# Two columns of the second feed-forward weight fetched by rows, around the first weight, in a decode step with cached attention

## The chip, the cores and the metric

The kernel runs on one core of a Trainium2 chip. The metric is the device time of one execution in microseconds (us); lower is better. TensorE multiplies matrices, VectorE (DVE), ScalarE (ACT) and GpSimd (POOL) work element by element, and SyncE (SP) issues all the transfers between the main memory and the on-chip memory here. Sixteen DMA engines carry these transfers. The on-chip memory has 128 partitions, which below are also called rows, since a row of a packed weight lies in one partition.

## The reference

One decoding step for four sequences: an adaptive layer norm that is steered by `c`, attention over a cache of 4096 keys and values with 32 heads of 128, a second adaptive layer norm, and a feed-forward block with SiLU.

```python
mod = (_silu(c) @ w_mod).reshape(c.shape[0], 6, 1, -1)
sa, ca, ga, sb, cb, gb = (mod[:, 0], mod[:, 1], mod[:, 2], mod[:, 3], mod[:, 4], mod[:, 5])
h = _layernorm(x) * (1 + ca) + sa
q = (h @ wq)                                   # (4, 32, 1, 128) after the reshape
scores = einsum("bhqd,bhkd->bhqk", q, k_cache) * 128 ** -0.5
o = einsum("bhqk,bhkd->bhqd", softmax(scores), v_cache)
x = x + ga * (o.reshape(4, 1, 4096) @ wo)
h = _layernorm(x) * (1 + cb) + sb
x = x + gb * (_silu(h @ w1) @ w2)              # w1: 512 x 1792, w2: 1792 x 512
```

All numbers are 32-bit floats. The two caches are 256 MiB each and are read once.

## The kernel before

The work is cut into N = 32 steps; a step is four heads of one sequence. For each step the keys (8 MB) and the values (8 MB) come into the on-chip memory, each into one of three `Slot`s of 8 MB that go round. In a step, VectorE and GpSimd multiply the keys by the query (`mult`, L280) and VectorE sums them (`red`, L285); the largest score is found (`rowmax`, `bmax`, `negmax`), ScalarE takes the exponentials (`softexp`, L307), and the sum over the values is shared by GpSimd (`vmult`) and TensorE (`pv`, L348). In the last two steps `first(n)` is 0, so that `pv` takes all 32 groups of the values, 64 matmul instructions.

After the last step's `pv` the closing work follows, in this order on TensorE:

- `project_a()` (L423): the output projection of the first half of the heads, from `wat`, the first RA x D = 8192 elements of each row of the slot that holds `wo`.
- `gather(NT - 1, 1)` (its matmul is L375), then `project(TA, NT - 1)` (L428) with three blocks of `wot`, 6144 elements a row, then `spread(NT - 1)` on VectorE, and `project(NT - 1, NT)` (L428) with the last block, 2048 elements a row.
- L500 and L501 copy the sum, four small matmuls spread it (L504), the residual is added, and the second layer norm follows (`layernorm_mod`). `busy` (L497) issues matmuls whose result nobody reads.
- L515 multiplies by the first feed-forward weight `w1t`, SiLU follows, and VectorE transposes the result (L186).
- L525 multiplies by the second weight `w2t`: NI = 14 columns of D = 512 elements a row (256 KB each over the 128 rows), added up in one accumulator `pf`. Each column takes 8 matmul instructions in the trace. Then L529, L530 and the output's transfer (L531).

The tile framework runs with a manual schedule: each engine carries out its instructions in the order in which the program text issues them. Waits are derived from the data: an instruction that reads a part of a tile waits for the transfer that writes that part, and for the whole of this transfer.

All transfers are issued by SP, nearly all through the helper `fetch` (L85), which cuts a row at the given places and issues one transfer of 128 rows for each piece. Each transfer reports on a semaphore; eight of them go round, so SP issues a transfer only when the one eight places before it has landed. The transfers at the end are, in the order of issue: the last keys in two halves, the last values, `wo` in three pieces (8192, 6144 and 2048 elements a row; the call is in the loop, L444), then `w12`, in which `w1` (4 x 1792 elements a row) and `w2` (14 x 512) lie one behind the other. `w12` (L476) comes in nine pieces: the first three quarters of `w1`, its last quarter, and `w2` by columns 0 to 4, 5 to 7, 8 and 9, and then one each for 10, 11, 12 and 13. The slot of `w12` is free once the last keys have been summed, and its first transfers are issued at 1278.9 us.

Of the kernel before, what the change touches and what calls it, by code (L numbers as in the profile page):

```python
# [17 lines left out]
def kernel(  # L18
# [10 lines left out]
    nc = tc.nc  # L29
    P = 128  # L30
    B, H, S, Dh = kc.shape
    D = wo.shape[1] * P // (H * Dh)
    F = w12.shape[1] * P // (2 * D)
# [8 lines left out]
    RA = Dh // QA  # L42
# [5 lines left out]
    R = Dh // QW  # L48
    NK = D // P
    NI = F // P  # L50
# [7 lines left out]
    SLOT = NJ * Dh  # L58
# [7 lines left out]
    def psum(shape, tag, bufs):  # L66
        return ps.tile(shape, F32, tag=tag, name=tag, bufs=bufs)
# [15 lines left out]
    def fetch(t, src, *cuts):  # L83
        for lo, hi in zip(cuts, cuts[1:]):
            nc.sync.dma_start(t[:, lo:hi], src[:, lo:hi])  # L85

    kt, vt = {}, {}

# [6 lines left out]
    def load_k(n, *cuts):  # L95
        load(kt, kc, "k", n, *cuts)

    def load_v(n):
        load(vt, vc, "v", n)
# [143 lines left out]
    for k in range(NK):  # L243
        for ch in range(H * Dh // CW):
            i, g = divmod(ch, G)
            nc.tensor.matmul(
                pq[i][W * g : W * (g + 1), :], hT[:, k, :], wqt[:, k, ch * CW : (ch + 1) * CW],
                start=k == 0, stop=k == NK - 1,
# [4 lines left out]
    for i in range(2):  # L253
        for u in range(HP):
# [3 lines left out]
                start=i + u == 0, stop=i == 1 and u == HP - 1,  # L258
# [6 lines left out]
    def make_qb(n):  # L265
        if n % B == 0:
            m = work.tile([P, B, Dh], F32, tag="o", name=f"qm{n}", bufs=1)
            for b in range(B):
                nc.scalar.activation(m[:, b, :], qn, AF.Copy, scale=sel[:, n + b : n + b + 1])  # L269
            p = psum([P, B, Dh], "q", 2)  # L270
            nc.tensor.matmul(p, blk.rearrange("p i x -> p (i x)"), m, start=True, stop=True)  # L271
            for b in range(B):
                qb[n + b] = p[:, b, :]
        qw[n] = work.tile([P, Dh], F32, tag="qw", name=f"qw{n}")
        nc.scalar.activation(qw[n], qb[n], AF.Copy)  # L275
# [3 lines left out]
    def mult(eng, src, n, lo, hi):  # L279
        eng.tensor_mul(  # L280
            kt[n][:, lo:hi, :], kt[n][:, lo:hi, :], src[n].unsqueeze(1).to_broadcast([P, hi - lo, Dh])
        )

    def red(n, lo, hi):
        nc.vector.tensor_reduce(sc[n][:, lo:hi], kt[n][:, lo:hi, :], axis=AX.X, op=ALU.add)  # L285

    def rowmax(n):
        nm[n] = work.tile([P, 1], F32, tag="rm", name=f"rm{n}")
        nc.vector.tensor_reduce(nm[n], sc[n], axis=AX.X, op=ALU.max)  # L289

    def bmax(n):
        p = psum([P, P], "mx", 2)
        nc.tensor.transpose(p, nm[n].to_broadcast([P, P]), ident)  # L293
        nm[n] = p

    def negmax(n):
        m = work.tile([P, HP], F32, tag="hx", name=f"hx{n}")
        nc.vector.tensor_reduce(m, nm[n].rearrange("p (i x) -> p i x", i=HP), axis=AX.X, op=ALU.max)  # L298
        nc.vector.tensor_mul(m, m, hn)
        nm[n] = work.tile([P, 1], F32, tag="nm", name=f"nm{n}")  # L300
        nc.vector.tensor_reduce(nm[n], m, axis=AX.X, op=ALU.add)  # L301

    def softexp(n):
        t, b = divmod(n, B)
        if b == 0:
            rs[t] = work.tile([P, B], F32, tag="rs", name=f"rs{t}")
        nc.scalar.activation(sc[n], sc[n], AF.Exp, bias=nm[n], accum_out=rs[t][:, b : b + 1])  # L307
        for h in range(2):
            f = first(n) if h == 0 else 0
            m = HG - f  # L310
            nc.gpsimd.tensor_mul(  # L311
                pz[h][:, f * W : HG * W].rearrange("p (g x) -> p g x", g=m)[:, :, E:].rearrange("p g (i j) -> p g i j", i=HP),
                sc[n][:, JJ * (HG * h + f) : HG * JJ * (h + 1)].rearrange("p (g j) -> p g j", j=JJ)
                .unsqueeze(2).to_broadcast([P, m, HP, JJ]),
                hm.unsqueeze(1).unsqueeze(3).to_broadcast([P, m, HP, JJ]),
            )

    def first(n):
        return NV // JJ if n < N - 2 else 0
# [9 lines left out]
    def vsum(n):  # L329
        t, b = divmod(n, B)  # L330
        q, a = divmod(b, 2)
        o = (1 - a) * E
        nc.tensor.matmul(  # L333
            po[t, q][0:W, :], hs[:, o : o + W], vt[n][:, :JJ, :].rearrange("p j d -> p (j d)"),
            start=False, stop=a == 1,
        )
# [42 lines left out]
    def norm(t):  # L379
        p = psum([P, B], "mx", 2)  # L380
        if t < TA:
            g = slice(W * t, W * (t + 1))
            nc.tensor.matmul(p[g], b8.rearrange("p i x -> p (i x)"), rs[t], start=True, stop=True)
            rd[t] = work.tile([P, B, QA], F32, tag="ra", name="ra", bufs=1)
            m = work.tile([P, B], F32, tag="dx", name="dx")
            nc.vector.reciprocal(m[g], p[g])
            nc.vector.tensor_mul(
                rd[t][g], m[g].unsqueeze(2).to_broadcast([W, B, QA]),
                dqm[g].unsqueeze(1).to_broadcast([W, B, QA]),
            )  # L390
            return
        nc.tensor.matmul(p, blk.rearrange("p i x -> p (i x)"), rs[t], start=True, stop=True)
        m = work.tile([P, B], F32, tag="dx", name="dx")
        nc.vector.tensor_mul(m, p, xm)
        rd[t] = work.tile([P, 2], F32, tag="rd", name="rd")
        nc.vector.tensor_reduce(rd[t][:, 0:1], m, axis=AX.X, op=ALU.add)
        nc.vector.reciprocal(rd[t][:, 1:2], rd[t][:, 0:1])

    def spread(t):
        if t < TA:  # L400
            g = slice(W * t, W * (t + 1))
            v = work.tile([P, B, QA, RA], F32, tag="o", name="v", bufs=1)
            nc.vector.tensor_mul(
                v[g], od[t][g].rearrange("p b (q r) -> p b q r", q=QA),
                rd[t][g].unsqueeze(3).to_broadcast([W, B, QA, RA]),
            )
            nc.vector.tensor_reduce(oa[g], v[g].rearrange("p b q r -> p r b q"), axis=AX.X, op=ALU.add)
            return
        on = work.tile([P, R, QW], F32, tag="lnu", name="on", bufs=1)
        nc.vector.tensor_scalar(  # L410
            on, od[t].rearrange("p (x r) -> p r x", r=R), rd[t][:, 1:2], None, op0=ALU.mult
        )
        ot = work.tile([P, R, W], F32, tag="o", name="ot", bufs=1)
        nc.vector.transpose(ot, on)
        nc.vector.tensor_copy(oz[:, t - TA], ot[:, :, :B])
# [19 lines left out]
    for n in range(N):  # L435
        t, b = divmod(n, B)
        if n < N - 2:
            load_k(n + 1)
        elif n == N - 2:
            load_k(n + 1, 0, NJ // 2, NJ)  # L440
        else:
            so = Slot("wo")
            wat, wot = so.take(RA, D), so.take(NT - TA, R, D)
            fetch(so.t, wo, 0, RA * D, SLOT - R * D, SLOT)  # L444
        sc[n] = work.tile([P, NJ], F32, tag="sc", name=f"sc{n}")
        if n + 1 < N:
            mult(nc.gpsimd, qw, n, 0, NA)
            mult(nc.vector, qb, n, NA, NJ)
            make_qb(n + 1)
            if n and first(n - 1):  # L450
                vsum(n - 1)
            red(n, NA, NJ)
        else:
            for lo in (0, NJ // 2):
                mid, hi = lo + NL // 2, lo + NJ // 2
                mult(nc.gpsimd, qw, n, lo, mid)
                mult(nc.vector, qb, n, mid, hi)
                red(n, mid, hi)
        if n + 1 < N:
            red(n, 0, NA)  # L460
        else:
            for lo in (0, NJ // 2):
                red(n, lo, lo + NL // 2)
        rowmax(n)
        bmax(n)
        negmax(n)
        if t and b == 1:
            spread(t - 1)
        softexp(n)
        if n + 1 < N:  # L470
            load_v(n + 1)
        else:
            s2 = Slot("w12")
            w1t = s2.take(NK, F)
            w2t = s2.take(NI, D)
            fetch(s2.t, w12, 0, 3 * F, *(NK * F + i * D for i in (0, 5, 8, 10, 11, 12, 13, 14)))  # L476
        if b == B - 1:
            norm(t)
        vmult(n)
        pv(n)  # L480
        if n and b == 0:
            gather(t - 1, 1)
        if b == 2:
            gather(t, 0)
# [28 lines left out]
    for k in range(NK):  # L513
        for g in range(G):
            nc.tensor.matmul(  # L515
                ph[W * g : W * (g + 1), :], h2T[:, k, :], w1t[:, k, g * FG : (g + 1) * FG],
                start=k == 0, stop=k == NK - 1,
# [2 lines left out]
    silu2(hid, th, ph)  # L520
    transposed(hidT, hid, NI)
    pf = psum([P, P], "po", 2)
    for i in range(NI):
        for g in range(G):
            nc.tensor.matmul(  # L525
                pf[W * g : W * (g + 1), :], hidT[:, i, :], w2t[:, i, g * P : (g + 1) * P],
                start=i == 0, stop=i == NI - 1,
            )
    nc.vector.tensor_mul(y, gb, pf)  # L529
    nc.vector.tensor_add(y, y, x1)  # L530
# [43 lines left out]
```

## Time and profile before

| | |
|---|---|
| time, median of 3 runs | 1320.01 us (1319.31 to 1320.38) |
| the profiled execution's own time | 1319.19 us |
| its span in the profile | 1317.4 us |
| busy: TensorE, VectorE, ScalarE, GpSimd | 377.2, 1017.4, 51.5, 842.8 us |
| moved by the DMA engines | 567.65 MB, mean 431 GB/s |
| mean granted TensorE clock | 0.611 of full speed |

Times in the profile count from the span's start. "L423 PE" is line 423 of the kernel on TensorE's matmul side, PEld its weight loads, PEldq the sequencer in front of them, SPq SP's own queue. A row of the timeline has start, duration, engine, line, operation, output <- input, shape and count, and in brackets the engine's idle time before it and what ended it. A row of busy time by stretches has the stretch, its length, busy time and count of PE, PEld, DVE, ACT and POOL, the granted TensorE clock, the busy share of the 16 DMA engines and the GB/s. A row of issues has the transfer, how often, its size and the time from issue to landing. A row of waits has who waited for whom, the total, the number of times and the longest. A piece of the chain of work that ended last has start, duration and what it was.

### The profile page before, as it was taken

The page shows a single profiled execution, that of the slowest core. Times are in us where ns is not written, and L with a number is a line of the kernel's source. Part 1 is how long each engine was busy: PE and PEld are TensorE (multiplying, and loading weights), DVE is VectorE, ACT ScalarE, POOL GpSimd, SP SyncE. Part 2 cuts the span into 40 slices and gives each one's busy share as a digit, 9 for nine tenths or more (in the row PEclk, how much of TensorE's full clock was granted, in tenths as well). Part 3 has the DMA queues.
Part 4 walks back from the last instruction along what each step waited for, and adds up shares of the span by engine and source line. Part 5 has one row for each costly group of instructions (what it writes and reads, how often), then busy time and mean ns, then how long its engine had stood idle before and what let it go on. Part 6 is the DMA issues. An engine that isn't in the chain of part 4 may idle for free.

```text
span 1317.4 us, 5420 instructions
## 1 busy us (share of the span) xinstructions
PE 377.2 (29%) x2114; PEld 94.6 (7%) x2114; DVE 1017.4 (77%) x361; ACT 51.5 (4%) x164; POOL 842.8 (64%) x227
## 2 busy tenths in 40 slices
PE   3421133223123232212332321332331233222138
PEld 1100000000000000000000000000000000000013
DVE  2378877777987777898777788777779877777982
ACT  1100000000000000000000000000000000000001
POOL 0236687666678666668866666876666787666650
PEclk9755566665566666556666555666655666655569
DMA  9999999999999999999999999999999999999998
GB/s 414 440 420 444 432 430 438 428 438 437 424 442 438 424 438 436 432 438 433 432 436 430 433 440 430 434 436 434 436 430 438 434 431 436 432 432 438 424 434 342
DMA packets 11433, 567.65 MB, mean 431 GB/s; under 512 B 1280, under 2 KB 1296, under 8 KB 2192
## 3 DMA queue, kind: packets, MB, share of 16 engines
q1 hardware_dynamic: 11408, 567.31, 99.5%
q8 instruction: 17, 0.28, 0.1%
q14 instruction: 8, 0.07, 0.0%
HBM read 567.30 MB, written 0.01 MB: 431 GB/s over the span
## 4 chain that ended last, share of the span: by engine, by line
DVE 36%; DMA 35%; POOL 19%; another core or an unknown queue 3%; PE 3%; issue 2%; ACT 1%; DVEq 0%; POOLq 0%; ACTq 0%
DMA k<-in_A_k_cache_dram 31%; DVE sc L285 21%; DVE k L280 14%; POOL v L327 9%; POOL v L323 8%; DMA w<-in_B_w_dram 3%; PE po L333 2%; DMA wm<-in_head_dram 1%; POOL pz L311 1%; POOL k L280 1%; ACT sc L307 1%; PE mx L293 1%; DVE hx L298 0%; DVE rm L289 0%
## 5 line engine op out<-in xcount | busy, mean ns | idle before, releaser
L285 DVE TENSOR_REDUCE sc<-k 128x88 f32<-128x11264 f32 (+2 forms) x66 | 553.1, 8422 | 1.1
L280 DVE TENSOR_TENSOR k<-k,q 128x11264 f32<-128x11264 f32 (+1 forms) x33 | 378.4, 11468 | 214.7 <-DMA k<-in_A_k_cache_dram 214.7
L280 POOL TENSOR_TENSOR k<-k,qw 128x5120 f32<-128x5120 f32 (+1 forms) x33 | 356.3, 10799 | 39.1 <-DMA k<-in_A_k_cache_dram 39.1
L311 POOL TENSOR_TENSOR pz<-sc,hm 128x128 f32<-128x128 f32 (+1 forms) x64 | 31.5, 512 | 376.9 <-ACT sc L307 376.9
L348 PE MATMUL po<-v,pz 128*32 128x512 f32 x1568 | 241.9, 781 | 44.9 <-POOL pz L311 44.8
L327 POOL TENSOR_TENSOR v<-v 128x2048 f32<-128x2048 f32 (+2 forms) x90 | 244.6, 2718 | 7.1
L323 POOL TENSOR_TENSOR v<-v,sc 128x4096 f32<-128x4096 f32 x30 | 210.9, 7031 | 0.0
L293 PE MATMUL mx<-ident,rm 128*128 128x128 f32 x32 | 14.5, 453 | 612.7 <-DVE rm L289 612.7
L333 PE MATMUL po<-v,hs 128*32 128x512 f32 x60 | 57.4, 1060 | 235.0 <-POOL v L327 235.0
L348 PEld LDWEIGHTS po<-v,pz 128*32 128x32 f32 x1568 | 56.6, 139 | 208.6 <-issue 156.2
L293 PEld LDWEIGHTS mx<-ident,rm 128*128 128x128 f32 x32 | 5.8, 181 | 664.9 <-issue 503.3
L307 ACT ACTIVATE sc<-sc,nm 128x128 f32<-128x128 f32 x32 | 12.8, 401 | 667.9 <-DVE nm L301 667.9
L275 ACT ACTIVATE qw<-q 128x128 f32<-128x128 f32 x32 | 8.9, 277 | 481.8 <-DVE k L280 454.2
L298 DVE TENSOR_REDUCE hx<-mx 128x4 f32<-128x128 f32 x32 | 9.3, 292 | 19.7 <-PE mx L293 19.7
L333 PEld LDWEIGHTS po<-v,hs 128*32 128x32 f32 x60 | 5.4, 140 | 257.9 <-POOL v L327 257.9
L359 DVE TENSOR_TENSOR o<-po,jm 128x512 f32<-128x512 f32 x16 | 10.9, 682 | 8.1 <-PE po L348 8.1
L365 DVE TENSOR_REDUCE s<-o 128x128 f32<-128x512 f32 x16 | 16.7, 1043 | 0.6
L199 PE MATMUL q<-wm 128*32 128x512 f32 x48 | 8.8, 665 | 18.8 <-DVE wm L183 18.8
L269 ACT ACTIVATE qm<-qn,sel 128x128 f32<-128x128 f32 x32 | 10.2, 390 | 31.2 <-PE od L370 27.7
L271 PE MATMUL q<-qm,blk 128*128 128x512 f32 x16 | 8.7, 625 | 7.2 <-ACT qm L269 7.2
L189 POOL COPY wm<-wm 128x16 f32<-128x16 f32 x1 | 0.2, 211 | 16.0 <-DMA wm<-in_head_dram 16.0
L183 DVE SCALAR_TENSOR_TENSOR wm<-wm 128x16 f32<-128x16 f32 x1 | 0.2, 189 | 12.8 <-ACT wm L182 12.8
(113 smaller groups left out, 153.2 us busy)
## 6 DMA issues: line engine op xcount, KB each, us to landing
k<-in_A_k_cache_dram SPq DMA_DIRECT2D x2, 4096.0 KB, 22.3
wm<-in_head_dram SPq DMA_DIRECT2D x1, 6160.0 KB, 17.6
wo<-in_A_wo_dram SPq DMA_DIRECT2D x1, 4096.0 KB, 26.8
wo<-in_A_wo_dram SPq DMA_DIRECT2D x1, 3072.0 KB, 33.7
w<-in_B_w_dram SPq DMA_DIRECT2D x1, 2688.0 KB, 23.8
w<-in_B_w_dram SPq DMA_DIRECT2D x1, 1280.0 KB, 28.1
wo<-in_A_wo_dram SPq DMA_DIRECT2D x1, 1024.0 KB, 35.7
w<-in_B_w_dram SPq DMA_DIRECT2D x4, 256.0 KB, 17.5
```

The lines of the kernel that those rows point to most:

```text
L269: nc.scalar.activation(m[:, b, :], qn, AF.Copy, scale=sel[:, n + b : n + b + 1])
L280: eng.tensor_mul(kt[n][:, lo:hi, :], kt[n][:, lo:hi, :], src[n].unsqueeze(1).to_broadcast([P, hi - lo, Dh]))
L285: nc.vector.tensor_reduce(sc[n][:, lo:hi], kt[n][:, lo:hi, :], axis=AX.X, op=ALU.add)
L293: nc.tensor.transpose(p, nm[n].to_broadcast([P, P]), ident)
L307: nc.scalar.activation(sc[n], sc[n], AF.Exp, bias=nm[n], accum_out=rs[t][:, b : b + 1])
L311: nc.gpsimd.tensor_mul(pz[h][:, f * W : HG * W].rearrange("p (g x) -> p g x", g=m)[:, :, E:].rearrange("p g (i j) -> p g i j", i=HP), sc[n ...
L323: nc.gpsimd.tensor_mul(vt[n][:, :NV, :], vt[n][:, :NV, :], sc[n][:, :NV].unsqueeze(2).to_broadcast([P, NV, Dh]))
L327: nc.gpsimd.tensor_add(vt[n][:, :m, :], vt[n][:, :m, :], vt[n][:, m : 2 * m, :])
L333: nc.tensor.matmul(po[t, q][0:W, :], hs[:, o : o + W], vt[n][:, :JJ, :].rearrange("p j d -> p (j d)"), start=False, stop=a == 1,)
L348: nc.tensor.matmul(po[t, q][W * g : W * (g + 1), :], pz[h][:, o : o + W], vt[n][:, JJ * j : JJ * (j + 1), :].rearrange("p j d -> p (j d)") ...
L359: nc.vector.tensor_mul(o, po[t, q].rearrange("p (j d) -> p j d", j=JJ), jm.unsqueeze(2).to_broadcast([P, JJ, Dh]))
L365: nc.vector.tensor_reduce(s, o.rearrange("p j d -> p d j"), axis=AX.X, op=ALU.add)
```

## The change

Three places change.

1. A helper `by_rows` issues transfers of whole columns of `w2` by groups of rows: each transfer takes a number of consecutive rows of one column. Column 12 comes so in transfers of 30, 42, 36 and 20 rows, issued ahead of `w1`; column 13 in transfers of 52, 44, 18, 8 and 6 rows, issued behind `w1`. The other twelve columns follow as before in transfers of 128 rows, now cut as 0 to 2, 3 to 5, 6 and 7, and then one each for 8, 9, 10 and 11. In all, `w12` comes in 18 transfers instead of nine.
2. `wo` comes in two transfers (14336 and 2048 elements a row) instead of three (8192, 6144 and 2048).
3. L525 begins with columns 12 and 13 and then takes 0 to 11.

```diff
+    def by_rows(t, src, i, counts):
+        lo, c = 0, NK * F + i * D
+        for k in counts:
+            nc.sync.dma_start(t[lo : lo + k, c : c + D], src[lo : lo + k, c : c + D])
+            lo += k
...
-            fetch(so.t, wo, 0, RA * D, SLOT - R * D, SLOT)
+            fetch(so.t, wo, 0, SLOT - R * D, SLOT)
...
-            fetch(s2.t, w12, 0, 3 * F, *(NK * F + i * D for i in (0, 5, 8, 10, 11, 12, 13, 14)))
+            by_rows(s2.t, w12, NI - 2, (30, 42, 36, 20))
+            fetch(s2.t, w12, 0, 3 * F, NK * F)
+            by_rows(s2.t, w12, NI - 1, (52, 44, 18, 8, 6))
+            fetch(s2.t, w12, *(NK * F + i * D for i in (0, 3, 6, 8, 9, 10, 11, 12)))
...
-    for i in range(NI):
+    for i in (NI - 2, NI - 1, *range(NI - 2)):
         for g in range(G):
             nc.tensor.matmul(
                 pf[W * g : W * (g + 1), :], hidT[:, i, :], w2t[:, i, g * P : (g + 1) * P],
-                start=i == 0, stop=i == NI - 1,
+                start=i == NI - 2, stop=i == NI - 3,
             )
```

## The prediction, made before the changed kernel was run

> **What bounds the kernel now.** I read the page's DMA part first, then the chain that ended last, the timeline of the last 60 us, the issues and waits of the SP queue, and busy time by stretches of 3.41 us, the step in which the granted clock changes.
>
> ```profile
> DMA packets 11433, 567.65 MB, mean 431 GB/s; under 512 B 1280, under 2 KB 1296, under 8 KB 2192
> ```
> ```profile
> 1278.91 23.84 DMA w<-in_B_w_dram
> 1302.75 0.02 issue
> 1302.77 10.87 DMA w<-in_B_w_dram
> 1313.64 0.04 issue
> 1313.68 0.47 PE po L525 x8
> ```
>
> The bytes flow at 431 GB/s over the whole span, and the chain's last pieces are two transfers of the feed-forward weights: the stream of bytes sets the end. The last 256 KB land at 1313.64, TensorE starts on them 0.04 us later and needs 0.47 us. So up to 1278.9 nothing changes, and the case is decided in the last 40 us. What runs beside the stream there:
>
> ```profile
> 1281.87 8.55 PE L348 MATMUL po<-v,pz 128*32 128x512 f32 x64
> ...
> 1290.25 3.61 PE L423 MATMUL acc<-wo,oa 128*4 128x512 f32 x32
> ...
> 1293.79 0.49 PE L375 MATMUL od<-s,spick 128*128 128x128 f32 x2
> ...
> 1294.21 3.62 PE L428 MATMUL acc<-wo,oz 128*4 128x512 f32 x32
> ...
> 1297.89 0.42 DVE L500 COPY ac<-acc 128x256 f32<-128x256 f32 x1 [2.67 <-PE acc L428]
> ...
> 1303.17 4.29 PE L515 MATMUL q<-w 128*32 128x448 f32 x32 [0.17 <-DVE w L186]
> ...
> 1309.82 2.94 PE L525 MATMUL po<-w 128*32 128x128 f32 x96 [1.05 <-DVE w L186]
> ...
> 1313.68 0.43 PE L525 MATMUL po<-w 128*32 128x128 f32 x8 [0.21 <-DMA w<-in_B_w_dram]
> 1314.17 0.29 DVE L529 TENSOR_TENSOR w<-mod,po 128x128 f32<-128x128 f32 x1 [4.41 <-PE po L525]
> ```
>
> This is one string of dependent work: the last values' product (L348), project_a (L423), the last gather (L375), project (L428), the copy, layer norm, first feed-forward product (L515), second (L525). It is nearly as long as the stream. L525 waits for its activations until 1309.82 and only then for weights.
>
> How much room does that string have? With every weight there, L525 would take 13 columns of eight matmuls and a last one of 0.47. A stretch in which L525 is all that TensorE does gives the price of a column:
>
> ```profile
> 1308.80:1312.22 3.42, 2.40 (x88) 2.34 (x88) 0.94 (x1) 0.00 (x0) 0.00 (x0) 1.00 0.74 290
> ```
>
> 88 matmuls in 2.40 us are 0.218 us a column. 1309.82 + 13 x 0.218 + 0.47 = 1313.13, against the true end at 1314.15: **the string has 1.0 us of room**, no more.
>
> **The change, part by part.**
>
> *The first two transfers of wo become one.* project_a reads the first 8192 elements of a row of wo, and wot's first three blocks the next 6144. They came by two transfers and now come by one of 7 MB, and a transfer is waited for as a whole. When did the two land?
>
> ```profile
> wo<-in_A_wo_dram SPq DMA_DIRECT2D x1, 4096.0 KB, 26.8
> wo<-in_A_wo_dram SPq DMA_DIRECT2D x1, 3072.0 KB, 33.7
> ```
> ```profile
> 1259.84 0.80 SPq L85 DMA_DIRECT2D wo<-in_A_wo_dram  x2
> 1286.64 0.33 SPq L85 DMA_DIRECT2D w<-in_B_w_dram  x1
> 1293.91 0.33 SPq L85 DMA_DIRECT2D w<-in_B_w_dram  x1
> ```
> ```profile
> SPq L85 <- DMA wo<-in_A_wo_dram: 14.6, 3, 6.9
> ```
>
> Issued from 1259.84 on, the first lands at 1259.84 + 26.8 = 1286.6 and the second at about 1260.2 + 33.7 = 1293.9. The SP queue agrees: it holds each of its later issues until the transfer eight places earlier has landed, and it is freed at 1286.64 and again at 1293.91, 6.9 us after that issue. Before, project_a found its weights at 1286.6 and began right behind L348, at 1290.25. Now it waits for 1293.9. The bytes in front of it in the stream are the same, so I see nothing that makes the 7 MB land earlier: a start at 1293.9 + 0.04 instead of 1290.25, **+3.7 us**. TensorE takes its work in order, so L375, L428 and all that follows go with it. Less the 1.0 us of room, 2.7 us reach the end.
>
> *What the wait does to TensorE's clock.* L348 ends at 1290.4, so TensorE sits idle for 3.5 us, on an engine that ran at full clock here.
>
> ```profile
> 1257.60:1261.02 3.42, 2.58 (x26) 0.66 (x14) 3.42 (x1) 0.00 (x0) 3.42 (x2) 1.00 0.88 383
> 1261.02:1264.43 3.41, 0.00 (x0) 0.00 (x0) 3.41 (x2) 0.00 (x0) 3.41 (x1) 1.00 1.06 461
> 1264.43:1267.84 3.41, 0.00 (x0) 0.00 (x0) 3.38 (x2) 0.00 (x0) 2.89 (x1) 0.50 0.93 404
> ...
> 1281.50:1284.91 3.41, 3.31 (x18) 0.97 (x21) 0.48 (x3) 0.00 (x0) 0.89 (x2) 0.50 0.94 404
> 1284.91:1288.32 3.41, 3.41 (x36) 0.96 (x32) 0.00 (x0) 0.00 (x0) 0.00 (x0) 1.00 1.01 435
> ...
> 1298.56:1301.98 3.42, 2.42 (x21) 1.76 (x18) 1.70 (x7) 1.60 (x3) 0.00 (x0) 1.00 0.95 405
> 1301.98:1305.39 3.41, 3.24 (x18) 1.32 (x20) 0.92 (x3) 1.60 (x3) 0.00 (x0) 0.50 1.00 423
> ```
>
> The eighth column is the granted clock. A stretch's clock follows from how busy the stretch before it was: after 0.00 us busy it fell to 0.50, after 2.42 it fell too, after 2.58 it stayed. At 0.50 the same product gets 18 matmuls through a stretch instead of 36. A gap of 3.5 us lies over two stretches of 3.41, which together keep 6.83 - 3.5 = 3.3 us of work; so at least one has 1.7 or less, under the 2.42 that lost the clock. If the emptier one is the second, the whole next stretch of project_a and L428 runs at half clock: 3.41 / 2 = 1.7 us lost. If it is the first, only the busy part of the next is slowed: 0.85 us or somewhat more. I take 1.7, because a stretch like the one at 1281.50 is regained at once; bounds 0 (clock kept) and 3.4 (two stretches).
>
> The rule that speaks for the lower bound is the Trainium skill's, in "TensorE: Matmul & The Clock Gate", section "Part 1: The HAM clock gate": half rate comes after at least one idle window of some 3.4 us, and the windows run free. Read strictly, a gap of 3.5 us holds a whole window in few cases, and the sum would be +2.8 us, 1322.8, instead of +4.5. The trace differs: the stretch from 1298.56 had 21 matmuls and the clock was lost.
>
> *The later stretches.* L515 already ran its first part at half clock (the stretch from 1301.98). Where the steps fall after the shift is open: fully granted it saves about (3.41 - 1.2) / 2 = 1.1 us, and wholly in a slow stretch it loses (3.41 - 2.2) / 2 = 0.6 more. I take 0.
>
> *Columns 12 and 13 by rows, nine transfers for two.* Four stand ahead of w1 and five behind. Their bytes are the same 512 KB. SP issues nine transfers more, at 0.33 us each, in stretches in which it waits anyway (14.6 us in the row above). As every issue waits for the landing eight earlier, and wo has one transfer fewer, the five behind w1 wait for wo's two and for row transfers, the transfer of columns 3 to 5 for w1's first part (1302.75, the chain's row). From there columns 3 to 11 remain, 2.36 MB, 5.5 us at 431 GB/s, behind 1.8 us of issue (the output's own issue to landing, below): 1310.1 even if the stream ran dry then. That is before 1313.64, so nothing in it; a stall of some engines lies under the late string.
>
> ```profile
> out_dram<-w SPq DMA_DIRECT2D x1, 8.0 KB, 1.8
> ```
>
> *What the rows do to the stream's end.* It ends raggedly:
>
> ```profile
> 1309.00:1310.00 1.00, 0.18 (x8) 0.18 (x12) 0.77 (x1) 0.00 (x0) 0.00 (x0) 1.00 0.93 369
> 1310.00:1311.00 1.00, 1.00 (x44) 1.00 (x40) 0.00 (x0) 0.00 (x0) 0.00 (x0) 1.00 0.70 270
> 1311.00:1312.00 1.00, 1.00 (x46) 1.00 (x40) 0.00 (x0) 0.00 (x0) 0.00 (x0) 1.00 0.58 223
> 1312.00:1313.00 1.00, 0.77 (x24) 0.32 (x16) 0.00 (x0) 0.00 (x0) 0.00 (x0) 1.00 0.33 125
> 1313.00:1313.64 0.64, 0.43 (x8) 0.16 (x8) 0.00 (x0) 0.00 (x0) 0.00 (x0) 1.00 0.17 45
> ```
>
> The ninth column is the share of the 16 DMA engines that still work. Missing are 0.07 + 0.30 + 0.42 + 0.67 + 0.64 x 0.83 = 2.0 us: that much earlier the stream would end if all engines ended together, and evening them is all that unequal rows can bring. The other bound is a row transfer that leans on one engine; it stands as a rival. Between them I take 0 for the end: with L525 starting at about 1314 or later, its weights are there whether the stream ends at 1311.6 or 1314. If the cover of the late string were gone, this term would be -2.0 to some +1.
>
> *Order of L525.* Columns 12 and 13 go first; the count is the same. Column 12 has four transfers to wait for and column 13 five.
>
> ```profile
> L525 PEldq EVENT_SEMAPHORE  x1: 51/51/51, 1307.9 to 1307.9; - x1
> ```
>
> Seven waits more at 0.051 are 0.36 us at most, of which the first column's lie in TensorE's wait for the activations: I take 0.15, bounds 0 and 0.36.
>
> **Sum.** 3.7 - 1.0 + 1.7 + 0 + 0 + 0.15 = +4.5 us. The profiled execution took 1319.19 us, its span 1317.4 and 1.8 around it; the sum is 1323.7 on that. The median shown, 1320.01, lies 0.8 above it, so I state 1324.4.
>
> **Rivals.**
>
> *The late string keeps its clock.* As the forecast, but the stretches share the gap so that none loses the clock, or L515 gains back what project_a lost. For: the limit lies between 2.42 and 2.58 busy by the rows, and the trace's busy time is modelled. Against: half the gap in each leaves 1.7. Time: 1320.0 + 2.8 = 1322.8, which sits at the 0.2% line. The Trainium skill's rule on the clock, read strictly, gives the same. Chance 0.16.
>
> *The stream still decides: not slower.* The 7 MB would have to land by 1290.25 + 1.0 = 1291.3; then the delay is inside the room, the end is the stream's, and evening the engines brings 0 to 2.0 us: 1318.0 to 1320.0. For: at 1309 to 1313.64 the engines end over more than 4 us, so the bytes lie there long on most engines before the last one reports; a stream that reaches wo more even lands it up to 2.0 us earlier. Against: that needs 2.6, nothing ahead of wo is altered, and the releases at 1286.64 and 1293.91 say when. By the Trainium skill's "DMA: Bandwidth & Descriptors", section "Rules for kernel authors", transfers to disjoint partitions are no gain over one of 128 partitions, which speaks against this rival too; no row shows a transfer of fewer rows in the stream. Chance 0.12.
>
> *Row transfers lean on few engines.* A 256 KB column costs 16 engines 0.6 us at 431 GB/s, 0.076 us a row with eight rows each. Two columns all on one engine would be 256 x 0.076 = 19 us there: some 1336 after the 3 us of cover. Eight engines used alike would cost 16 x 0.076 = 1.2 us and stay hidden. Only a transfer on three engines or fewer decides. Nothing in the trace tells; chance 0.04.
>
> **How the numbers follow.** The forecast has 0.68, with its own range from the clock's bounds: +3.2 to +6.3, 1323.0 to 1326.3. For 8 in 10 the range takes in most of the clock-keeping rival and leaves out the other two: 1321.9 to 1326.6. The limit of what can be told is 0.2%, 2.6 us, so slower means above 1322.6: 0.68 + about 0.10 of the first rival + 0.04 = 0.82; same is the rest of it and most of the stream's case, 0.15; faster 0.03.
>
> **What the changed profile would show.** Right: L423's weight loads wait on wo and start near 1293.9; L348 and L423 are separated by 3.5 us; a stretch of 0.50 clock in L423 or L428; L500 near 1303, not 1298; L525 starts near 1315, waits for no weights, and the chain's last DMA piece is wo. The stream may end earlier than 1313.6 without anyone noticing. Wrong: L423 starts by 1291.3, or the chain still ends in a transfer of w, or its last column lands after 1316.

## The result: 1324.2 us against 1319.8, slower by 0.29%

| | median | lowest to highest | runs |
|---|---|---|---|
| kernel before | 1319.79 us | 1319.19 to 1320.49 | 9 |
| changed kernel | 1324.21 us | 1321.65 to 1325.00 | 9 |

The ratio is 1.0029, with a 95% interval from 1.0019 to 1.0040; ratios, here and below, are of the means and not of the medians. The profiled execution of the changed kernel took 1324.31 us (span 1322.5), 5.12 us more than that of before. Line numbers have moved: the last values' product is L354 (L348 before), project_a L429 (L423), project L434 (L428), the first feed-forward product L524 (L515), the second L534 (L525), and L538 is L529. Runs made from the kernel before keep its numbers.

The chain that ended last, in the changed kernel (start, duration, what):

```profile
1261.39 33.62 DMA wo<-in_A_wo_dram
1295.02 0.04 issue
1295.06 4.97 PE acc L429 x32
1300.03 0.42 PE od L381 x2
1300.45 3.59 PE acc L434 x32
...
1309.34 4.31 PE q L524 x32
...
1315.96 3.31 PE po L534 x112
1319.27 0.02 issue
1319.29 0.30 DVE w L538
```

Before, the last two long pieces were transfers of `w12`. Now the last transfer in the chain is `wo`, and from 1295.06 on everything is the string of dependent work, to the end. L534 runs its 112 matmuls in one go: no wait for weights is left in it. The timeline of TensorE shows the gap in front:

```profile
1282.30 9.68 PE L354 MATMUL po<-v,pz 128*32 128x512 f32 x64
1295.06 4.97 PE L429 MATMUL acc<-wo,oa 128*4 128x512 f32 x32 [3.09 <-DMA wo<-in_A_wo_dram]
```

And the stretches between the steps of the granted clock (eighth column; the first pair of columns is the stretch and its length, then TensorE's busy time):

```profile
1291.01:1294.42 3.41, 0.96 (x12) 0.06 (x4) 1.71 (x2) 0.00 (x0) 0.00 (x0) 1.00 0.92 334
1294.42:1297.84 3.42, 2.78 (x16) 0.55 (x20) 0.00 (x0) 0.00 (x0) 0.00 (x0) 0.50 1.06 340
1297.84:1301.25 3.41, 3.41 (x33) 0.82 (x28) 0.69 (x3) 0.00 (x0) 0.00 (x0) 1.00 0.96 405
1304.67:1308.08 3.41, 2.41 (x20) 1.70 (x19) 1.70 (x7) 1.60 (x3) 0.00 (x0) 1.00 1.00 313
1308.08:1311.49 3.41, 3.31 (x18) 1.46 (x21) 0.92 (x3) 1.67 (x3) 0.00 (x0) 0.50 0.98 359
```

The stretch with the gap has 0.96 us of work, and the next one, in which project_a runs, gets half the clock. A second reading is in the last columns: the DMA engines are busy, share about 1, and yet move only 313 to 359 GB/s in four of the five stretches, where the kernel before had 404 to 435 in those shown from 1281.50 to 1305.39. The stream's end, in the changed kernel, microsecond by microsecond:

```profile
1312.00:1313.00 1.00, 1.00 (x16) 0.28 (x12) 0.00 (x0) 0.00 (x0) 0.00 (x0) 1.00 1.06 408
1313.00:1314.00 1.00, 1.00 (x12) 0.48 (x5) 0.00 (x0) 0.27 (x1) 0.00 (x0) 1.00 0.97 363
1314.00:1315.00 1.00, 0.90 (x9) 0.71 (x7) 0.66 (x2) 0.27 (x1) 0.00 (x0) 1.00 0.60 227
1315.00:1316.00 1.00, 0.04 (x4) 0.04 (x7) 0.90 (x1) 0.00 (x0) 0.00 (x0) 1.00 0.19 72
```

By the updates of the semaphores, the last column reports from its 16 engines between 1313.89 and 1316.28; before, it was between 1309.78 and 1313.64. The ends are closer together (2.4 us instead of 3.9), but all of them are later. That is hidden under the string, and the experiments had to bring it to light.

### The profile page after: what moved, and what is told of

It is laid out like the page before. It is cut to its first block, busy times and chain, and to the rows that moved or that the text cites. A ratio compares the mean times of both kernels' runs of the same rounds, so it can differ in the third digit from the quotient of the medians.

```text
span 1322.5 us, 5431 instructions
## 1 busy us (share of the span) xinstructions
PE 376.9 (28%) x2114; PEld 94.5 (7%) x2114; DVE 1017.3 (77%) x361; ACT 51.5 (4%) x164; POOL 842.8 (64%) x227
## 4 chain that ended last, share of the span: by engine, by line
DMA 38%; DVE 35%; POOL 19%; PE 5%; issue 2%; ACT 1%; DVEq 0%; SPq 0%; POOLq 0%; ACTq 0%
DMA k<-in_A_k_cache_dram 33%; DVE sc L291 20%; DVE k L286 13%; POOL v L333 9%; POOL v L329 8%; DMA wq<-in_A_wq_dram 3%; DMA wo<-in_A_wo_dram 3%; PE po L339 2%; POOL pz L317 1%; POOL k L286 1%; PE po L354 1%; ACT sc L313 1%; PE mx L299 1%; PE q L252 1%; PE acc L429 0%
## 5 line engine op out<-in xcount | busy, mean ns | idle before, releaser
L354 PE MATMUL po<-v,pz 128*32 128x512 f32 x1568 | 241.0, 779 | 44.8 <-POOL pz L317 44.7
L354 PEld LDWEIGHTS po<-v,pz 128*32 128x32 f32 x1568 | 56.5, 139 | 207.8 <-issue 155.4
L213 DVE TENSOR_TENSOR wm<-q,hm 64x256 f32<-64x256 f32 (+1 forms) x8 | 4.1, 548 | 8.8 <-PE q L205 7.8
```

The costliest lines, as they stand in the source:

```text
L354: nc.tensor.matmul(po[t, q][W * g : W * (g + 1), :], pz[h][:, o : o + W], vt[n][:, JJ * j : JJ * (j + 1), :].rearrange("p j d -> p (j d)") ...
```

## The experiments

The theory after the result: the late string, caused by the merge of `wo`, sets the end; the row transfers do harm of their own, which the string covers. The medians of the kernel before beside these runs were 1319.30 to 1319.54 us.

### wo in three transfers again

```diff
-            fetch(so.t, wo, 0, SLOT - R * D, SLOT)
+            fetch(so.t, wo, 0, RA * D, SLOT - R * D, SLOT)
```

> The changed kernel with wo in three transfers again, so that project_a waits for the first 4 MB alone; the row transfers and the new order stay. Theory (late string on the path, and under it a stream that the row transfers have made longer): project_a starts at about 1290.3 and the string is early again, but now the stream's end shows, which stood at 1316.3 in the changed kernel against 1313.6 before: 1321 to 1322.5 us, 1 to 2.5 above the kernel before. Rival 1 (the merge is all, the row transfers cost nothing): 1319.3 to 1320.3, no difference. Rival 2 (the row transfers even out the engines' ends): 1318.0 to 1319.3. Rival 3 (the merge is not the cause): still 1324.

Measured: 1321.98 us against 1319.34, ratio 1.0019 (1.0010 to 1.0028). TensorE's timeline in this run:

```profile
1290.31 3.61 PE L429 MATMUL acc<-wo,oa 128*4 128x512 f32 x32
...
1305.60 4.72 PE L524 MATMUL q<-w 128*32 128x448 f32 x32 [1.73 <-DMA w<-in_B_w_dram]
...
1312.67 3.37 PE L534 MATMUL po<-w 128*32 128x128 f32 x104 [1.04 <-DVE w L192]
1316.25 0.43 PE L534 MATMUL po<-w 128*32 128x128 f32 x8 [0.21 <-DMA w<-in_B_w_dram]
```

project_a is back at 1290.31, and still 2.6 us are lost: the last column of L534 now waits for its weights until 1316.25, against 1313.68 before. Rivals 1 and 2 fall. The row transfers even out nothing that counts; they make the stream 2.6 us longer. What stands beside them in the stream is late too: the last piece of `wo` lands at 1297.97 instead of 1296.41, by SP's releases, and L524 waits 1.73 us for the first weight.

### The merge alone

```diff
 (the kernel before)
-            fetch(so.t, wo, 0, RA * D, SLOT - R * D, SLOT)
+            fetch(so.t, wo, 0, SLOT - R * D, SLOT)
```

> The kernel before with the merge of wo's first two transfers alone. Theory: project_a waits for about 1293.9, +3.7, less 1.0 of room, and one stretch of half clock, up to 1.7: 1322.7 to 1325, about 1324.2, as much as the whole change. Rival (the row transfers and their issues cost the time): 1319.5 to 1320.5.

Measured: 1322.35 us (1320.92 to 1324.24) against 1319.34, ratio 1.0023 (1.0014 to 1.0032). The merge alone costs 3.0 us, so it is a cause in its own right, but the size is under the expected range. The profile of one of the quickest executions (1320.94 us) says why, in its timeline

```profile
1294.05 3.62 PE L423 MATMUL acc<-wo,oa 128*4 128x512 f32 x32 [3.19 <-DMA wo<-in_A_wo_dram]
...
1306.97 3.21 PE L515 MATMUL q<-w 128*32 128x448 f32 x32 [0.60 <-DVE w L186]
...
1312.54 3.26 PE L525 MATMUL po<-w 128*32 128x128 f32 x112 [1.04 <-DVE w L186]
```

and in its stretches:

```profile
1289.06:1292.47 3.41, 1.80 (x20) 0.27 (x12) 1.50 (x2) 0.00 (x0) 0.00 (x0) 1.00 0.81 347
1292.47:1295.89 3.42, 1.84 (x20) 0.54 (x24) 0.21 (x1) 0.00 (x0) 0.00 (x0) 1.00 1.00 426
1295.89:1299.30 3.41, 3.41 (x34) 0.84 (x26) 0.84 (x3) 0.00 (x0) 0.00 (x0) 1.00 0.98 423
```

The start at 1294.05 is the predicted one, 3.8 us late. The gap fell half into each of two stretches, 1.80 and 1.84 us of work stayed in them, and the clock was kept; L515 ran at full clock too and gained 1.1 us. The eleven times lie in three groups, two near 1320.9, six from 1322.1 to 1322.8, three from 1324.0 on: the same code. What this profile shows is what the first rival described. That the steps of the clock make the three groups is a guess that no run shows: only one of the eleven has a trace.

### Work in the gap

```diff
     (the helper `busy` and its tile now stand ahead of this)
+    busy(14)
     project_a()
     gather(NT - 1, 1)
```

> The changed kernel with 14 of the idle products that nobody reads (28 matmul instructions of about 0.107 us at full clock) between the last values' product and project_a, in the gap that TensorE waits for wo. Theory (the half clock in project_a is a term of its own, 1.4 to 1.7 us): 1322.4 to 1323.2, and a granted clock of 1.00 throughout project_a and L434. Rival (the clock costs nothing at the end): 1324.2 as the changed kernel.

Measured: 1323.40 us against 1319.34, ratio 1.0027 (1.0017 to 1.0037). Its timeline and stretches (the numbers have moved again: L525 is here the first feed-forward product):

```profile
1294.19 3.62 PE L429 MATMUL acc<-wo,oa 128*4 128x512 f32 x32 [0.63 <-DMA wo<-in_A_wo_dram]
...
1307.37 5.46 PE L525 MATMUL q<-w 128*32 128x448 f32 x32
```
```profile
1301.70:1305.11 3.41, 2.15 (x20) 1.33 (x16) 1.72 (x7) 1.67 (x2) 0.00 (x0) 1.00 0.97 329
1305.11:1308.52 3.41, 3.13 (x16) 2.19 (x20) 1.32 (x5) 1.75 (x3) 0.00 (x0) 0.50 1.00 329
1308.52:1311.94 3.42, 3.42 (x24) 0.88 (x20) 0.00 (x0) 0.00 (x0) 0.00 (x0) 0.50 0.98 376
```

project_a takes 3.62 us instead of 4.97, as expected. The median is 0.8 us under the changed kernel's (0.4 when each is taken against the runs of before beside it), 0.2 above the expected range, and the two ratios lie within each other's intervals: no gain at the end is shown. In this execution the clock is lost later, in the thin work of the layer norm, and the first feed-forward product takes 5.46 us, so most of the gain is given back there. `wo` also landed 0.9 us earlier than in the changed kernel's profile, which the idle products don't touch. The clock is a term inside an execution, and one that moves.

### wo cut in the middle

```diff
 (the kernel before)
-            fetch(so.t, wo, 0, RA * D, SLOT - R * D, SLOT)
+            fetch(so.t, wo, 0, RA * D, SLOT)
```

> The kernel before with wo in two transfers cut in the middle, 8192 and 8192 elements a row: project_a is early as before, but project waits for the last byte of wo, 1296.4 instead of 1294.2. Theory (1.0 us of room in the string): +2.2 - 1.0 = +1.2, and in some executions a stretch of half clock for the gap of 2.2 us: 1320.3 to 1322.5, about 1321. Rival (the string has 2.2 us of room or more): 1319.0 to 1320.0.

Measured: 1320.30 us against 1319.54, ratio 1.0004 (0.9995 to 1.0013): by the times alone no verdict. The profiled execution's span is 1318.6, 1.2 over that of before, and its timeline shows the expected sum:

```profile
1296.31 3.62 PE L428 MATMUL acc<-wo,oz 128*4 128x512 f32 x32 [0.92 <-DMA wo<-in_A_wo_dram]
...
1305.27 4.37 PE L515 MATMUL q<-w 128*32 128x448 f32 x32 [0.32 <-DVE w L186]
...
1312.01 3.26 PE L525 MATMUL po<-w 128*32 128x128 f32 x112 [1.05 <-DVE w L186]
```

L428 starts 2.1 us later than before (1294.21), L525 2.2 us later (1309.82), and the end comes 1.2 us later: in this execution the string's room is 1.0 us. The other executions don't all agree: five of the eleven took 1319.18 to 1319.71 us, no more than the kernel before, and six took 1320.30 to 1321.75. Without a trace of one of the five, what spared them stays open.

### Whole columns at the same places

```diff
 (wo in three transfers)
-            by_rows(s2.t, w12, NI - 2, (30, 42, 36, 20))
+            by_rows(s2.t, w12, NI - 2, (P,))
...
-            by_rows(s2.t, w12, NI - 1, (52, 44, 18, 8, 6))
+            by_rows(s2.t, w12, NI - 1, (P,))
```

> As the run with wo in three transfers, but column 12 and column 13 come each in one transfer of 128 rows at the same two places. Theory (few rows in a transfer make the stream slower, not the place in the order): the stream keeps 420 to 440 GB/s in the stretches of the two columns and ends at 1313.3 to 1314, 1319.3 to 1320.3 us. Rival (the place in the order, or issues that wait for the landing eight earlier, cost the time): 1321 to 1322.5, as with rows.

Measured: 1319.94 us against 1319.34, ratio 1.0004 (0.9995 to 1.0012). Order and place cost nothing that can be told. From 1292 to 1300, where column 12 passes, the stream keeps its 434 GB/s, and the last column of L534 waits until 1313.64,

```profile
1292.00:1300.00 8.00, 7.45 (x68) 2.32 (x59) 2.24 (x8) 1.67 (x2) 0.00 (x0) 1.00 1.02 434
```
```profile
1313.64 0.43 PE L534 MATMUL po<-w 128*32 128x128 f32 x8 [0.25 <-DMA w<-in_B_w_dram]
```

as in the kernel before (1313.68). So it is the transfers by rows.

### Rows of 32, neighbours or every fourth

Two runs, each with four equal transfers of 32 rows a column (and wo in three), which differ in the rows alone:

```diff
-            by_rows(s2.t, w12, NI - 2, (30, 42, 36, 20))
+            by_rows(s2.t, w12, NI - 2, (W, W, W, W))
...
-            by_rows(s2.t, w12, NI - 1, (52, 44, 18, 8, 6))
+            by_rows(s2.t, w12, NI - 1, (W, W, W, W))
...
 (second run, in by_rows, with m = 4 transfers)
-            nc.sync.dma_start(t[lo : lo + k, c : c + D], src[lo : lo + k, c : c + D])
+            nc.sync.dma_start(t[lo::m, c : c + D], src[lo::m, c : c + D])
```

> As the run with wo in three transfers, but both columns come in four transfers of 32 neighbouring rows each, two rows for each of 16 engines. Theory A (neighbouring rows are what slows the stream, since all engines then write into a narrow band of partitions): again 300 to 350 GB/s in the stretches of the two columns, a stream that ends at 1315 to 1316.5, 1321 to 1322.5 us. Theory B (the unequal number of engines, 6 to 15 of them, is what slows it): 420 GB/s and more, 1319.3 to 1320.3.

> As the run with four transfers of 32 rows, but each transfer takes every fourth row, so that it reaches over all 128 partitions; the number of transfers, their sizes, engines and waits are the same. Theory A (narrow band of partitions): 420 GB/s and more in those stretches, 1319.3 to 1320.4 us. Rival (the number of transfers and the issues that wait for the landing eight earlier): as with neighbouring rows, 1321 to 1322.5.

Measured: 1322.76 us against 1319.54 with neighbouring rows, 0.3 above the expected range, ratio 1.0025 (1.0015 to 1.0035), so transfers that all use 16 engines do not help. With every fourth row 1322.82, ratio 1.0026 (1.0016 to 1.0036), which by the time alone would refute theory A. The traces tell another tale: by the semaphores' updates, with neighbours the last column lands at 1316.94, with every fourth row at 1313.78. TensorE's last rows, first with neighbours, then with every fourth row:

```profile
1316.98 0.43 PE L534 MATMUL po<-w 128*32 128x128 f32 x8 [0.16 <-DMA w<-in_B_w_dram]
```
```profile
1314.74 3.28 PE L533 MATMUL po<-w 128*32 128x128 f32 x112 [1.05 <-DVE w L191]
```

In the second run the stream was as quick as before; the time went elsewhere. Its VectorE timeline:

```profile
1302.47 0.35 DVE L240 SCALAR_TENSOR_TENSOR w<-lnu,lnr,mod 128x128 f32<-128x128 f32 x1
1306.43 0.40 DVE L191 STREAM_TRANSPOSE w<-w 128x128 f32<-128x128 f32 x1 [3.61 <-DMA w<-in_B_w_dram]
```

The transpose in front of the first feed-forward product waits 3.6 us for a transfer of `w12`, though it touches none of its data: its result h2T lies behind the weights in the same slot. That the wait derived for a write to every fourth row of the slot reaches that far is a reading, which the next run tries.

### Every fourth row, the end's tiles in a slot of their own

```diff
+    s3 = Slot("late")
-    x1, hg, y = (s2.take(P) for _ in range(3))
-    h2T, hid, th, hidT = s2.take(NK, W), s2.take(FG), s2.take(FG), s2.take(NI, W)
+    x1, hg, y = (s3.take(P) for _ in range(3))
+    h2T, hid, th, hidT = s3.take(NK, W), s3.take(FG), s3.take(FG), s3.take(NI, W)
```

> As the run with every fourth row, but the small tiles of the end (x1, hg, y, h2T, hid, th, hidT) lie in the slot of the last values and not in that of w12, so that VectorE's transpose for the first feed-forward product no longer waits for the row transfers, as it did there until 1306.43. Theory (neighbouring rows slow the stream, and the run with every fourth row was held up by that wait alone): stream at 400 GB/s and more, end at 1313.3 to 1314, 1319.3 to 1320.4 us. Rival (transfers of 32 rows cost time wherever they lie): 1321 or more.

Measured: 1319.73 us against 1319.30, ratio 1.0003 (0.9994 to 1.0012). The transpose follows L240 without a wait, at 1303.01. With that wait gone, eight row transfers cost nothing that can be told. In the profiled execution the last column lands at 1314.23, 0.2 past the expected range; the last values, ahead of the change, were 0.5 late there too.

### Which side: read near and write far, and the opposite

```diff
 (every fourth row, own slot; the host lays out the last two columns' rows to match)
-            nc.sync.dma_start(t[lo::m, c : c + D], src[lo::m, c : c + D])
+            nc.sync.dma_start(t[lo::m, c : c + D], src[lo * W : (lo + 1) * W, c : c + D])
 (or)
+            nc.sync.dma_start(t[lo * W : (lo + 1) * W, c : c + D], src[lo::m, c : c + D])
```

> As the run with every fourth row and tiles in their own slot, but each transfer reads 32 neighbouring rows in memory and writes them to every fourth partition; the host lays the rows of the last two columns in another order for it. Theory A (the narrow band of partitions that is written slows the stream): fast, 1319.3 to 1320.4 us, the last column at 1313.3 to 1314. Theory B (neighbouring rows in memory slow the reading): 1321 to 1323, the last column at 1315.5 or later.

> The opposite: each transfer reads every fourth row in memory and writes 32 neighbouring partitions. Theory A (narrow band of partitions that is written): slow, 1321 to 1323 us, the last column at 1315.5 or later and 300 to 350 GB/s where the two columns pass. Theory B (neighbouring rows in memory): fast, 1319.3 to 1320.4.

Measured: 1319.61 us, ratio 1.0001 (0.9992 to 1.0010), for neighbouring rows read and every fourth partition written; 1323.03 us, ratio 1.0027 (1.0017 to 1.0038), for the opposite, both against 1319.30. The last columns land at 1313.84 and 1317.55. It is the writing side. One stretch of each kernel, from 1292 to 1300, in which column 12 passes (the last column is GB/s). The kernel before:

```profile
1292.00:1300.00 8.00, 7.45 (x68) 2.37 (x60) 2.25 (x8) 1.63 (x2) 0.00 (x0) 1.00 1.00 428
```

The changed kernel:

```profile
1292.00:1300.00 8.00, 4.94 (x33) 0.89 (x33) 1.71 (x2) 0.00 (x0) 0.00 (x0) 0.79 0.98 342
```

Its rows with wo in three transfers:

```profile
1292.00:1300.00 8.00, 6.46 (x58) 1.42 (x50) 1.61 (x5) 0.35 (x1) 0.00 (x0) 1.00 1.03 363
```

Four times 32 neighbouring rows:

```profile
1292.00:1300.00 8.00, 7.45 (x71) 1.80 (x63) 2.39 (x6) 0.77 (x2) 0.00 (x0) 1.00 1.01 353
```

Every fourth row, own slot:

```profile
1292.00:1300.00 8.00, 7.45 (x71) 2.21 (x60) 2.27 (x7) 1.33 (x2) 0.00 (x0) 1.00 1.02 433
```

Read near, write far:

```profile
1292.00:1300.00 8.00, 7.45 (x70) 1.82 (x62) 2.44 (x6) 0.70 (x2) 0.00 (x0) 1.00 1.02 429
```

Read far, write near:

```profile
1292.00:1300.00 8.00, 7.46 (x70) 1.63 (x62) 2.76 (x6) 0.26 (x1) 0.00 (x0) 1.00 1.04 355
```

The busy share is about 1 in all seven. Wherever a transfer writes neighbouring partitions, the engines are as busy and move 15 to 20% less. The single packets say the same. A packet of 2 KB that starts between 1293 and 1297 took 84 ns with whole columns and with every fourth row, 98 ns in the median (103 in the mean) in the changed kernel. Packets of the 128-row transfers under way at that time slow down with them: those of 8 KB, the size of `wo`'s last piece, from 309 to 391 ns, and those of 21 KB, the size of `w1`'s first, from 799 to 1106.

The Trainium skill, in "SBUF — State Buffer", section "Door 1: The DMA port swizzle", states that DMA bandwidth depends on how many of the memory's 16 ports the partitions reach, and that partitions 0 to 31 reach 8. The last two runs agree with it: 355 GB/s against 429, with the same number of transfers, rows and engines. No run counts the ports themselves.

No run beat the kernel before.

## Why the prediction was right, and where it was not

*The merge and the wait.* Right. The predicted start of project_a was 1293.9 + 0.04; with the merge alone it was 1294.05, with the filled gap 1294.19. In the changed kernel's profile it is 1295.06, 1.1 us later than predicted. Of that, 0.4 is there before the change can act (L354 starts at 1282.30 instead of 1281.87, and the last values land at 1277.42 instead of 1276.97). The other 0.7 lies in the last engines' share of `wo`, at a time when the quicker engines already write rows of column 12; but the run with the filled gap has the same transfers and landed in time, so how much of it belongs to the rows stays open.

*The room.* Right in the profiles: 1.0 us was worked out from 88 matmuls in 2.40 us. The changed kernel needed 3.31 us from the start of L534 to its end, where the prediction had 13 x 0.218 + 0.47 = 3.30, and the run with wo cut in the middle took 1.0 us of a delay of 2.2 us away; five executions of that run took no longer than the kernel before, so the profile of one does not speak for all.

*The clock.* The term was right in kind and somewhat large in size: 4.97 - 3.61 = 1.36 us in the profile, for 1.7 predicted; the gap was 3.1 us and not 3.5, since the product in front of it, L354, took 9.68 us and ended at 1291.98. The reason given for it failed. The prediction read a limit between 2.42 and 2.58 us of busy time off two rows, and so held that the clock must be lost. In the run with the merge alone two stretches with 1.80 and 1.84 kept it, while 2.41 lost it in the changed kernel. Even about the same busy time in the same layer norm goes both ways: 2.42 lost it in the kernel before, and the merge alone kept it after

```profile
1302.70:1306.10 3.40, 2.41 (x20) 1.97 (x19) 1.86 (x8) 1.51 (x3) 0.00 (x0) 1.00 1.00 424
```

where L515 then ran at full clock. The busy time of these rows does not tell when the clock goes, and no run here shows what does. The rival's mechanism exists, in that one profiled execution; the eleven executions spread over 3.3 us, and that the clock is the reason is argued and not shown.

*The rows.* This is the step that was mis-sized. "Between them I take 0 for the end", with -2.0 to some +1 if the cover were gone: it is +2.6 (the run with wo in three). The prediction looked at how many engines a transfer uses and not at where it writes. Its bound of 1310.1 for the stream's end also let the first part of w1 land at 1302.75 as before; it landed at 1305.51, and the last column at 1316.28. It came to no harm since the late string covers it. By the count of semaphore updates the row transfers used 15, 14, 12, 10 and 13, 11, 9, 8, 6 engines: the rival of few engines was wrong, and the sign named for a failure, a last column after 1316, was there at 1316.28 without deciding anything.

*Order and issues.* Right: whole columns at the same places and eight transfers by every fourth row cost nothing that can be told, and L534 paid nothing for its extra waits (0.15 predicted).

*The sum.* In the profile: +4.81 for the start, +1.36 for the clock, -1.0 for the room make 5.2, and 5.12 was measured; predicted was +4.5. The medians differ by 4.4. Two figures do not follow from the terms: 1320.01 + 4.5 is 1324.5, where 1324.4 is stated, and with the clock kept the sum is +2.85, where the forecast's own range begins at +3.2.

The two harms are 3.0 and 2.6 us alone and 4.4 together, not 5.6: they run side by side, and the later end counts. In the changed kernel's profile the last column lands at 1316.28, 2.5 us before L534 comes to it, so there the string alone decides. Why 4.4 and not the merge's 3.0 is open; the ratios, 1.0029 and 1.0023, lie within each other's intervals, so it may be the spread between executions.

## What to carry to other kernels

When two transfers become one, ask what reads the first part: it now waits for the last byte. Here, behind a deep queue, the two landings lay 7.3 us apart, and the reader started 3.8 us later. When one kernel has two ends of nearly equal length, work out the room between them first; a harm on the shorter one is invisible until the longer one is mended, so undo the parts one by one. Where a transfer takes only some of the rows, try spreading them over all partitions, which cost nothing that could be told here, and keep out of its slot what others need early.

## What was not expected of the hardware

- Writing to neighbouring partitions slows the engines' other transfers too: 342 to 363 GB/s instead of 428 to 434 over 8 us, for a column of 256 KB, at a busy share of about 1. Why the others slow down too, no run shows.
- The ends of a transfer on its 16 engines lie apart by 1.1 us in the first transfer of the kernel before and by 3.9 us in the last. The spread grows in steps; most of them follow a 16 KB packet in the queue of instructions, which takes about 0.9 us. That the packet is the cause is not tested.
- In a gap of just over 3 us in front of project_a the granted clock was lost in one profiled execution (the changed kernel, 3.09 us idle) and kept in another (the merge alone, 3.19 us).
